# Attention's chain, a group's factor and the weight pieces moved in a one-core attention and expert kernel

## The chip, the core and the metric

One NeuronCore of a Trainium2 chip runs the whole program. Its engines are TensorE (PE, the matmuls), VectorE (DVE), ScalarE (ACT), GpSimd (POOL) and SyncE (SP, which issues nearly all DMAs here). Each engine executes its own instructions strictly in their order and waits on semaphores for the others. The metric is the device time of one execution in microseconds, the median of several runs.

## What is computed

```python
q_s = softmax(q over the 64 features of a head)
k_s = softmax(k over the 576 tokens)
x = q_s @ (k_s.T @ v)                            # 8 batches x 8 heads, 576 tokens, 64 features
xn = x / sqrt(mean(x * x) + 1e-6) * rms_g        # x as 4608 tokens x 512
y = (silu(xn @ w_gate) * (xn @ w_val)) @ w_out   # 512 -> 1536 -> 512
h = max(y @ w1, y @ w2, y @ w3)                  # 512 -> 768
out = h @ w_out2                                 # 768 -> 512
```

Everything is float32. A large product is made of three matmuls of rounded operands: the operand is split into a high part (a cast on ACT) and a low part (the difference on DVE), and high x high, low x high and high x low are added in PSUM.

## The kernel before

The 4608 tokens are nine groups of 512 (index g from 0 to 8; the last holds the tails of the 8 batches). Heads are taken in four pairs p. For each group and each of 12 feature blocks f, `iteration(g, nxt, f)` makes a gate product pg and a value product pv, 12 matmuls each (lines 598 to 600), a tanh of pg on ACT (948), the gate on DVE (949) and h on DVE (958); h goes to HBM. A group's products need its x split into xh and xl; a group's iterations therefore also do the attention of the next groups:

- the softmax of q. In groups 0 and 1 q is held by token, and `q_exp` runs eight exponentials of 128x64 on ACT with the row maximum as bias and the sum as accumulator (418). From group 2 on q is also loaded by feature (`load_by_feature`, into the tile qT): `q_exp` makes the statistics, which go through HBM (`put_stat`, `spread_stats`), `q_softmax` subtracts and multiplies on POOL with an exponential on ACT between (384 to 386), and `q_by_feature` splits the result into qh (ACT) and ql (DVE, line 100).
- `k_max`, `k_exp` (transpose pb, subtraction, exponential) and `make_kv` (pk, ten matmuls in line 453, then the scaling to kv_raw in 463 and its split).
- `make_x`: the product px of q and kv (496 to 498), scaled by the gain on ACT, squared, and the squares added on POOL (515).
- the group's factor: `token_rstd` sums the squares (548) and makes z, one over the root mean square, by three Newton steps on DVE (551 to 556). Groups 1 and 2 (`COMPACT`) spread z over the partitions with four transposes (`spread_rstd`, 571), later ones through HBM (`read_rstd`, into the tile zb of rooms_o). `normalise` multiplies x by it (580), `split_x` splits it.

Which chain step falls in which iteration is set by `turn_of(g, p)` (400), a number that counts pairs of iterations, and by the `due()` lists in `iteration`: `due(n)` holds the (g, p) whose turn is n pairs ahead. Within that a scheduler fixes the order on each engine when the program is built; the DMAs of SP stay in program order.

Beside all that, `second.advance` prepares the second layer's weights: it loads float64 words, joins them to float32 (`join`, ACT and DVE), sums them (`sums`, DVE) and writes them in quarters, called pieces below (`quarter` and `split`: a cast on ACT in line 274, a subtraction on POOL in 275, a write to w_dram by SP). It is called once per iteration from group 1 on; pieces are written in f = 0 to 9 only, except in the last group. What is left then, 13 pieces, is done by `mixture_out` (732 to 1000 us), the output stage that applies w_out by quarters with operands split in the same way (o_xh, o_xl and the like).

Of the kernel before, what the change touches and what calls it, by code (L numbers as in the profile page):

```python
# [8 lines left out]
F32 = mybir.dt.float32  # L9
# [17 lines left out]
BY_FEATURE = 2  # L27
NF1 = 12
# [26 lines left out]
def attention_moe_moe(ctx: ExitStack, tc: tile.TileContext, q, qt, k, kt, v, w1, w1_out, rms_g, w2, w2_out, out):  # L55
# [68 lines left out]
    eps = one.tile([P, LINE], F32, tag="eps", name="eps")[:, 0:1]  # L124
    nc.gpsimd.memset(eps, EPS_RMS)
# [77 lines left out]
    class Ahead:  # L203
# [5 lines left out]
        def __init__(self):  # L209
# [7 lines left out]
            self.loaded, self.st, self.now, self.apart = 0, [], 0, False  # L217
            self.issued, self.turn, self.spots = [], False, []
# [45 lines left out]
        def split(self, src, dst, name):  # L264
            if self.apart:
                self.turn = not self.turn
                t = two.tile([P, 2, N // 2], F32R, tag=("t", "qT")[self.turn], name=name, bufs=1)
            elif self.spots:
# [21 lines left out]
        def advance(self, f, last):  # L290
# [4 lines left out]
            self.apart = f is None  # L295
            room = 4 if last else 3
            while self.steps:
                step, args = self.steps[0]
                if step == self.join and self.now < self.issued[args[0]] + 2:
                    return  # L300
                writes = step == self.quarter
                cost = 0 if step == self.release else 1 if writes else 2
                if cost > room or writes and not last and f > 9:
                    return
# [94 lines left out]
    def turn_of(g, p):  # L399
        return NF1 // 2 * (g - 1) + p - (g > BY_FEATURE)  # L400

# [7 lines left out]
    def q_exp(g, p):  # L409
        qm = two.tile([P, 24], F32, tag="qm", name=f"qm_{g}_{p}")[:, 0:8]  # L410
        nc.vector.tensor_reduce(qm, q_t[g, p], axis=AX.X, op=ALU.max)
        if g < BY_FEATURE:
# [7 lines left out]
        qmax[g, p] = qm  # L420
        nc.gpsimd.tensor_sub(q_t[g, p], q_t[g, p], qm.unsqueeze(2).to_broadcast([P, 8, 64]))  # L421
        nc.scalar.activation(q_t[g, p], q_t[g, p], AF.Exp)

    def q_divide(g, p):
        qs = qsum.pop((g, p))
        nc.vector.tensor_scalar(qs, qs, EPS_SM, None, op0=ALU.add)
# [21 lines left out]
    def make_kv(g, p):  # L448
# [12 lines left out]
        for j in range(2):  # L461
            s = slice(64 * j, 64 * j + 64)
            nc.vector.tensor_scalar(raw[s, s], pk[s, s], rs[s, 0:1], None, op0=ALU.mult)
# [317 lines left out]
    def mixture_out(pr):  # L781
# [13 lines left out]
        for i, n in enumerate(OUT_ORDER1):  # L795
# [25 lines left out]
            if pr < 3 and i in (2, 4, 5, 6):  # L821
                second.advance(None, True)
# [24 lines left out]
    def iteration(g, nxt, f):  # L847
# [41 lines left out]
        if not odd:  # L889
            for t in due(-1):  # L890
                make_x(*t)
# [12 lines left out]
        else:  # L904
            for t in due(2):
                put_stat(*t, 0, qmax[t])
                load_second(*t)
# [9 lines left out]
            for t in due(0):  # L917
                q_by_feature(*t)
        if nxt is not None and nxt >= BY_FEATURE:
# [4 lines left out]
            if f == 10:  # L924
# [24 lines left out]
        nc.vector.scalar_tensor_tensor(t, t, 1.0, pg, op0=ALU.add, op1=ALU.mult)  # L949
        if ahead:  # L950
# [12 lines left out]
        if nxt in COMPACT and f == (10 if nxt < BY_FEATURE else at):  # L963
# [362 lines left out]
```

## Time and profile before

| | us |
|---|---|
| median of three runs | 1525.76 (1524.75 to 1528.61) |
| profiled execution | 1527.82, its span 1526.0 |
| TensorE busy | 1484.5 (97%) |
| DVE, ACT, POOL busy | 1060.2 (69%), 609.0 (40%), 447.6 (29%) |

A profile row names the engine, the line of the kernel, what is written from what, and in brackets how long the engine stood idle before and who released it. TensorE does its work in a fixed order, so its brackets show where the time goes that isn't matmul. The granted clock is a share of full speed; 0.5 is 1.2 GHz and 1.0 is 2.4 GHz.

### The profile page before, as it was taken

The numbers are of one execution on the slowest core, as the hardware profiler recorded it, in microseconds if no ns is written. First come the engines' busy times: TensorE is split into PE (matmuls) and PEld (weight loads), VectorE is DVE, ScalarE is ACT, GpSimd is POOL, SyncE is SP. The second block draws the span as 40 slices with busy tenths as digits, with TensorE's granted clock in tenths as the row PEclk, the third lists the DMA queues.
The fourth block names the chain that finished last, engine by engine and source line by source line (L and its number), as shares of the span: only waits on it lengthen the run. The fifth ranks groups of instructions, "written<-read, shape, count | busy, mean of one in ns | idle before, by whom it ended". The sixth has DMA issues, their size and how long they took to land. (4 is left out here: it accounts for less than half of the span.)

```text
span 1526.0 us, 19735 instructions
## 1 busy us (share of the span) xinstructions
PE 1484.5 (97%) x6692; PEld 1220.3 (80%) x6692; DVE 1060.2 (69%) x1777; ACT 609.0 (40%) x1197; POOL 447.6 (29%) x379
## 2 busy tenths in 40 slices
PE   5899999999999999999999999999999999999999
PEld 4687778887878788888867888888888888888887
DVE  6997585767576756473889989838848848847722
ACT  7754343434343433341554545413413413413311
POOL 0012443434334344441565764211111111111100
PEclk9999999999999999999999999999999999999999
DMA  8865786868686968789665154255485485485573
GB/s 273 292 196 175 224 240 197 250 213 238 201 250 210 246 195 231 238 279 348 223 235 186 60 199 174 106 199 201 165 323 199 170 321 196 167 297 202 171 264 104
DMA packets 159333, 330.30 MB, mean 216 GB/s; under 512 B 31104, under 2 KB 55680, under 8 KB 159232
## 3 DMA queue, kind: packets, MB, share of 16 engines
q1 hardware_dynamic: 155776, 322.74, 65.2%
q10 hardware_dynamic: 3456, 6.29, 1.1%
q8 instruction: 53, 0.87, 0.2%
q14 instruction: 48, 0.39, 0.1%
HBM read 246.42 MB, written 82.55 MB: 216 GB/s over the span
## 5 line engine op out<-in xcount | busy, mean ns | idle before, releaser
L1052 POOL TENSOR_TENSOR temps_wl<-temps_wl,temps_wh 128x512 f32<-128x512 f32 x36 | 48.2, 1338 | 348.8 <-ACT temps_wh L1051 282.0
L949 DVE SCALAR_TENSOR_TENSOR t<-t,pg 128x512 f32<-128x512 f32 x64 | 43.8, 684 | 62.4 <-ACT t L948 61.8
L275 POOL TENSOR_TENSOR rooms_o<-st,rooms_o 128x256 fp32r<-128x256 f32 x63 | 50.4, 807 | 113.8 <-ACT rooms_o L274 109.2
L421 POOL TENSOR_TENSOR q<-q,qm 128x512 f32<-128x512 f32 x28 | 31.1, 1112 | 175.4 <-PE pk L453 94.5
L1043 DVE TENSOR_TENSOR temps_wl<-temps_wl,p_a 128x512 f32<-128x512 f32 x72 | 49.1, 682 | 37.3 <-POOL temps_wl L1052 37.1
L1047 ACT COPY temps_wh<-p_G 128x512 f32<-128x512 f32 x36 | 21.1, 586 | 105.8 <-PE p_G L606 105.5
L604 PE MATMUL p_a<-x_wh,chunk 128*128 128x512 f32 x160 | 62.3, 389 | 0.0
L605 PE MATMUL p_a<-x_wl,chunk 128*128 128x512 f32 x160 | 62.3, 389 | 0.0
L606 PE MATMUL p_a<-x_wh,chunk 128*128 128x512 f32 x160 | 62.3, 389 | 0.0
L605 PE MATMUL p_a<-x_wh,chunk 128*128 128x512 f32 x160 | 62.2, 389 | 0.0
L604 PE MATMUL p_a<-x_wl,chunk 128*128 128x512 f32 x160 | 62.2, 389 | 0.0
L606 PE MATMUL p_a<-x_wl,chunk 128*128 128x512 f32 x160 | 62.2, 389 | 0.0
L958 DVE SCALAR_TENSOR_TENSOR h<-t,pv 128x512 f32<-128x512 f32 x66 | 45.0, 682 | 24.7 <-PE pv L600 22.3
L1049 DVE TENSOR_TENSOR temps_wl<-temps_wh,p_V 128x512 f32<-128x512 f32 x36 | 24.6, 683 | 43.9 <-PE p_V L606 43.9
L948 ACT ACTIVATE t<-pg 128x512 f32<-128x512 f32 x64 | 37.8, 590 | 39.4 <-PE pg L600 38.8
L755 POOL TENSOR_TENSOR h_X<-h_Y,h_X 128x512 f32<-128x512 f32 x24 | 41.7, 1747 | 28.4 <-DVE o_ql L100 12.4
L949 DVE SCALAR_TENSOR_TENSOR rooms_o<-rooms_o,pg 128x512 f32<-128x512 f32 x42 | 28.5, 678 | 28.8 <-ACT rooms_o L948 28.8
L757 POOL TENSOR_TENSOR h_Y<-h_W,h_Y 128x512 f32<-128x512 f32 x24 | 39.0, 1639 | 25.3 <-DMA h_W<-h_dram 24.9
L453 PEld LDWEIGHTS pk<-v,k 128*128 128x128 f32 x300 | 39.7, 200 | 7.5 <-issue 2.4
L453 PE MATMUL pk<-v,k 128*128 128x129 f32 x300 | 41.2, 285 | 4.4 <-DMA v<-in_v 2.2
L759 POOL TENSOR_TENSOR h_Z<-h_Z,h_X 128x512 f32<-128x512 f32 x24 | 40.0, 1685 | 11.0 <-DVE h_X L752 8.4
L948 ACT ACTIVATE rooms_o<-pg 128x512 f32<-128x512 f32 x42 | 24.8, 590 | 42.5 <-PE pg L600 42.4
(1227 smaller groups left out, 5001.7 us busy)
## 6 DMA issues: line engine op xcount, KB each, us to landing
chunk<-w_dram SPq DMA_DIRECT2D x112, 768.0 KB, 4.3
h_dram<-h SPq DMA_DIRECT2D x108, 256.0 KB, 3.6
w_dram<-rooms_o SPq DMA_DIRECT2D x95, 256.0 KB, 3.0
stat<-stats SPq DMA_DIRECT2D x112, 128.0 KB, 5.1
words<-in_w SPq DMA_DIRECT2D x24, 512.0 KB, 6.6
chunk<-w_dram SPq DMA_DIRECT2D x48, 256.0 KB, 3.7
k<-in_k SPq DMA_DIRECT2D x30, 320.0 KB, 4.5
v<-in_v SPq DMA_DIRECT2D x30, 320.0 KB, 5.9
```

What stands on the lines that cost most here:

```text
L275: nc.gpsimd.tensor_sub(t[:, 1, :], src, t[:, 0, :].bitcast(F32))
L453: nc.tensor.matmul(pk[:, 0 : P + 1], k_t[g, p][:, c, :], v_t[g, p][:, c, :], start=(c == 0), stop=(c == 4))
L604: nc.tensor.matmul(pt, ah, bh, start=first, stop=False, skip_group_check=onto)
L605: nc.tensor.matmul(pt, ah, bl, start=False, stop=False, skip_group_check=onto)
L606: nc.tensor.matmul(pt, al, bh, start=False, stop=last, skip_group_check=onto)
L755: nc.gpsimd.tensor_sub(x, y, x)
L759: nc.gpsimd.tensor_sub(z, z, x)
L948: nc.scalar.activation(t, pg, AF.Tanh, scale=0.5)
L949: nc.vector.scalar_tensor_tensor(t, t, 1.0, pg, op0=ALU.add, op1=ALU.mult)
L958: lows.append(nc.vector.scalar_tensor_tensor(h, t, 0.5, pv, op0=ALU.mult, op1=ALU.mult))
L1043: nc.vector.tensor_add(y, x, pt)
L1052: nc.gpsimd.tensor_add(w, u2, s5)
```

## The change

Four things are done. At the start, pairs 1 and 3 of group 0 (`AT_ONCE`) get their exponential in one instruction behind a subtraction on POOL, with the sum taken by a reduction on DVE; group 0's scaling to kv_raw goes from DVE to ACT; and a small exponential at the very start replaces a constant. From group 3 on `turn_of` is one smaller, and the lists are changed so that `make_x` stays where it was while `q_by_feature` comes half a pair earlier. Group 2's factor is spread and applied between pg and pv of f = 10 instead of at the end of f = 9. And pieces are written in every f, with none left to the output stage.

```diff
+AT_ONCE = ((0, 1), (0, 3))
...
-    eps = one.tile([P, LINE], F32, tag="eps", name="eps")[:, 0:1]
-    nc.gpsimd.memset(eps, EPS_RMS)
+    warm = one.tile([P, LINE], F32, tag="warm", name="warm")[:, 0:1]
+    nc.scalar.activation(warm, ones_f[:, 0:1], AF.Exp)
...
-        def advance(self, f, last):
+        def advance(self, last):
...
-                if step == self.join and self.now < self.issued[args[0]] + 2:
+                if step == self.join and (args[0] >= self.loaded or self.now < self.issued[args[0]] + 2):
                     return
-                writes = step == self.quarter
-                cost = 0 if step == self.release else 1 if writes else 2
-                if cost > room or writes and not last and f > 9:
+                cost = 0 if step == self.release else 1 if step == self.quarter else 2
+                if cost > room:
                     return
...
     def turn_of(g, p):
-        return NF1 // 2 * (g - 1) + p - (g > BY_FEATURE)
+        return NF1 // 2 * (g - 1) + p - 2 * (g > BY_FEATURE)
...
     def q_exp(g, p):
...
-        if g < BY_FEATURE:
+        if g < BY_FEATURE and (g, p) not in AT_ONCE:
...
+        if g < BY_FEATURE:
+            qsum[g, p] = two.tile([P, 8], F32, tag="qs", name=f"qs_{g}_{p}")
         nc.gpsimd.tensor_sub(q_t[g, p], q_t[g, p], qm.unsqueeze(2).to_broadcast([P, 8, 64]))
         nc.scalar.activation(q_t[g, p], q_t[g, p], AF.Exp)
 
     def q_divide(g, p):
         qs = qsum.pop((g, p))
+        if (g, p) in AT_ONCE:
+            nc.vector.tensor_reduce(qs, q_t[g, p], axis=AX.X, op=ALU.add)
...
-            nc.vector.tensor_scalar(raw[s, s], pk[s, s], rs[s, 0:1], None, op0=ALU.mult)
+            if g == 0:
+                nc.scalar.activation(raw[s, s], pk[s, s], AF.Copy, scale=rs[s, 0:1])
+            else:
+                nc.vector.tensor_scalar(raw[s, s], pk[s, s], rs[s, 0:1], None, op0=ALU.mult)
...
-            if pr < 3 and i in (2, 4, 5, 6):
-                second.advance(None, True)
...
         if not odd:
+            for t in due(-2):
+                if t[0] > BY_FEATURE:
+                    make_x(*t)
             for t in due(-1):
-                make_x(*t)
+                if t[0] > BY_FEATURE:
+                    q_by_feature(*t)
+                else:
+                    make_x(*t)
...
             for t in due(2):
                 put_stat(*t, 0, qmax[t])
-                load_second(*t)
+                if t[0] < NB:
+                    load_second(*t)
...
             for t in due(0):
-                q_by_feature(*t)
+                if t[0] == BY_FEATURE:
+                    q_by_feature(*t)
+                if t[0] == NB:
+                    load_second(*t)
...
-            if f == 10:
+            if f == 10 and nxt > BY_FEATURE:
                 for p in range(4):
                     normalise(nxt, p)
...
         nc.vector.scalar_tensor_tensor(t, t, 1.0, pg, op0=ALU.add, op1=ALU.mult)
+        if nxt == BY_FEATURE and f == 10:
+            spread_rstd(nxt)
+            for p in range(4):
+                normalise(nxt, p)
...
-        if nxt in COMPACT and f == (10 if nxt < BY_FEATURE else at):
+        if nxt == 1 and f == 10:
             spread_rstd(nxt)
...
-            second.advance(f, nxt is None)
+            second.advance(nxt is None)
```

What this does to the orders is shown at three places.

ACT at the start of the program; q_0 to wh_0_3 are the q of group 0's four pairs, k and wl hold k, pk and px are banks. Before:

```order
L418 ACTIVATE q_0_219,qs_0_269<-q_0_219,qm_0_267 128x64 x8
L418 ACTIVATE q_1_229,qs_1_287<-q_1_229,qm_1_285 128x64 x2
L444 ACTIVATE k_0_221<-k_0_221 128x640
L418 ACTIVATE q_1_229,qs_1_287<-q_1_229,qm_1_285 128x64 x6
L444 ACTIVATE k_1_231<-k_1_231 128x640
L418 ACTIVATE wh_0_2_239,qs_2_305<-wh_0_2_239,qm_2_303 128x64 x8
L444 ACTIVATE wl_0_2_241<-wl_0_2_241 128x640
L418 ACTIVATE wh_0_3_249,qs_3_327<-wh_0_3_249,qm_3_325 128x64 x8
L444 ACTIVATE wh_0_3_251<-wh_0_3_251 128x640
```

and after:

```order
L126 ACT_TABLE_LOAD
L126 ACTIVATE warm<-ones_f 128x1
L414 ACTIVATE q_0_219,qs_0_269<-q_0_219,qm_0_267 128x64 x8
L420 ACTIVATE q_1_229<-q_1_229 128x512
L444 ACTIVATE k_0_221<-k_0_221 128x640
L488 COPY qh_0_369<-pt_0_364 128x512
L444 ACTIVATE k_1_231<-k_1_231 128x640
L414 ACTIVATE wh_0_2_239,qs_2_298<-wh_0_2_239,qm_2_296 128x64 x8
L444 ACTIVATE wl_0_2_241<-wl_0_2_241 128x640
L464 ACTIVATE kv_raw_213<-pk_0_328,kr_0_336 64x64 x2
L488 COPY qrts<-pt_1_398 128x512
L420 ACTIVATE wh_0_3_249<-wh_0_3_249 128x512
```

Two pairs' eight exponentials became one instruction each, and group 0's kv_raw scalings (L464) stand on ACT among them.

PE around the factor of group 2 (z_2, the four transposes named rstd), in the iterations f = 9 and 10 of group 1. Before:

```order
L599 MATMUL pv_9_2060<-x_2_1398,wh_(1, 9)_1196 128x512
L600 MATMUL pv_9_2060<-x_2_1398,wl_(1, 9)_1215 128x512
L571 MATMUL rstd_2075<-ident,z_2_2033 128x128 x4
L453 MATMUL pk_0_2094<-v_0_223,k_0_1899 128x129 x5
L598 MATMUL pg_10_2124<-x_0_1390,wh_(1, 10)_1260 128x512
L599 MATMUL pg_10_2124<-x_0_1390,wh_(1, 10)_1260 128x512
```

and after, from the last matmuls of pg of f = 10:

```order
L601 MATMUL pg_10_2157<-x_2_1386,wh_(1, 10)_1248 128x512
L602 MATMUL pg_10_2157<-x_2_1386,wh_(1, 10)_1248 128x512
L603 MATMUL pg_10_2157<-x_2_1386,wl_(1, 10)_1267 128x512
L574 MATMUL rstd_2173<-ident,z_2_2071 128x128 x4
L601 MATMUL pv_10_2183<-x_0_1378,wh_(1, 10)_1248 128x512
L602 MATMUL pv_10_2183<-x_0_1378,wh_(1, 10)_1248 128x512
```

The transposes moved from ahead of pk and pg of f = 10 to behind that pg.

DVE at the end of the third group (g = 2): xraw is normalised (L580, after the change L583) with the factor in a tile of rooms_o, then split into the tiles x. Before:

```order
L949 SCALAR_TENSOR_TENSOR t_10_2877<-t_10_2877,pg_10_2864 128x512
L580 TENSOR_TENSOR xraw_0_2233<-xraw_0_2233,rooms_o_1432 128x512
L580 TENSOR_TENSOR xraw_1_2373<-xraw_1_2373,rooms_o_1432 128x512
L580 TENSOR_TENSOR xraw_2_2490<-xraw_2_2490,rooms_o_1432 128x512
L580 TENSOR_TENSOR xraw_3_2606<-xraw_3_2606,rooms_o_1432 128x512
L958 SCALAR_TENSOR_TENSOR h_10_2893<-t_10_2877,pv_10_2880 128x512
L376 TENSOR_REDUCE qs_2_2910<-q_2_2725 128x8
L443 TENSOR_TENSOR k_1_2771<-k_1_2771,pb_1_2915 128x640
L377 TENSOR_SCALAR qs_2_2910<-qs_2_2910 128x8
L100 TENSOR_TENSOR ql_0_2920<-qT_0_2721,qh_0_2919 128x512
L379 RECIPROCAL qr_2_2913<-qs_2_2910 128x8
L100 TENSOR_TENSOR x_0_2923<-xraw_0_2233,x_0_2923 128x512
```

and after:

```order
L960 SCALAR_TENSOR_TENSOR rooms_o_1421<-rooms_o_1421,pg_11_2990 128x512
L583 TENSOR_TENSOR xraw_0_2286<-xraw_0_2286,rooms_o_1420 128x512
L583 TENSOR_TENSOR xraw_1_2402<-xraw_1_2402,rooms_o_1420 128x512
L583 TENSOR_TENSOR xraw_2_2518<-xraw_2_2518,rooms_o_1420 128x512
L583 TENSOR_TENSOR xraw_3_2620<-xraw_3_2620,rooms_o_1420 128x512
L101 TENSOR_TENSOR x_0_2979<-xraw_0_2286,x_0_2979 128x512
L101 TENSOR_TENSOR x_1_2982<-xraw_1_2402,x_0_2979 128x512
L101 TENSOR_TENSOR x_1_2982<-xraw_2_2518,x_1_2982 128x512
L435 TENSOR_REDUCE km_3_2968<-kT_3_2911 128x1
L101 TENSOR_TENSOR x_2_2987<-xraw_3_2620,x_2_2987 128x512
L973 SCALAR_TENSOR_TENSOR h_11_3018<-rooms_o_1421,pv_11_3005 128x512
L101 TENSOR_TENSOR ql_1_3037<-rooms_o_1422,qh_1_3036 128x512
```

Normalise stood behind the gate of pg_10 and stands behind that of pg_11 now; ql of the next group's pair 1, which before came in f = 1 directly ahead of its product, follows h_11. At the end of the sixth group the order changes in the same way; at those of the fourth and fifth normalise stands one or two operations later than before, ahead of the gate of pg_11.

## Rows read from the trace of the kernel before

**Rows 1.** the page's busy time of each engine, its share of the span, and instructions
```profile
PE 1484.5 (97%) x6692; PEld 1220.3 (80%) x6692; DVE 1060.2 (69%) x1777; ACT 609.0 (40%) x1197; POOL 447.6 (29%) x379
```

**Rows 2.** what PE waited for: us in total, times, longest
```profile
PE rstd L571 <- DVE z L556: 5.2, 2, 2.7
...
PE px L497 <- DVE ql L100: 4.0, 7, 0.9
...
PE pv L548 <- POOL sacc L515: 1.0, 1, 1.0
```

**Rows 3.** stretches: PE, PEld, DVE, ACT, POOL busy; PEclk, DMA share, GB/s
```profile
0.00:60.00 60.00, 40.94 (x195) 31.17 (x196) 46.46 (x117) 45.25 (x147) 1.59 (x18) 0.94 0.82 279
60.00:115.00 55.00, 53.32 (x250) 41.68 (x248) 53.08 (x109) 35.06 (x86) 5.05 (x4) 1.00 0.71 224
118.00:121.00 3.00, 3.00 (x9) 2.30 (x8) 2.84 (x5) 2.24 (x4) 0.00 (x0) 0.51 0.23 87
193.00:196.00 3.00, 3.00 (x16) 2.91 (x14) 2.54 (x5) 1.67 (x3) 2.16 (x2) 0.52 0.83 300
```

**Rows 4.** timeline of ACT, POOL, DVE; start, duration, then the instruction; POOL's row is a summary
```profile
17.82 0.35 ACT L418 ACTIVATE wh<-wh,qm 128x64 f32<-128x64 f32 x1 [1.92 <-DVE qm L415]
...
20.49 0.72 ACT L444 ACTIVATE wh<-wh 128x640 f32<-128x640 f32 x1
...
L421 POOL TENSOR_TENSOR q<-q,qm x28: 1042/1045/1561, 96.7 to 594.1; 128x512 f32<-128x512 f32 x28
...
19.68 0.58 DVE L463 TENSOR_SCALAR kv_raw<-pk,kr 64x64 f32<-64x64 f32 x2
```

**Rows 5.** timeline of PE and DVE, 22 to 60 us
```profile
22.80 1.91 PE L494 MATMUL px<-qh,kv_raw 128*128 128x512 f32 x2
...
58.21 0.67 DVE L194 TENSOR_TENSOR wl_(1, 3)_772<-y,wh_(1, 3)_753 128x512 fp32r<-128x512 f32 x1
...
59.42 0.40 PE L600 MATMUL pg<-xh,wl_(1, 3)_772 128*128 128x512 f32 x1
```

**Rows 6.** timeline of DVE, POOL and PE, 114 to 118 us
```profile
114.32 1.20 DVE L556 SCALAR_TENSOR_TENSOR z<-a,z 128x4 f32<-128x4 f32 x1
...
116.43 0.15 DVE L556 SCALAR_TENSOR_TENSOR z<-a,z 128x4 f32<-128x4 f32 x1
...
114.23 1.27 POOL L386 TENSOR_TENSOR qT<-qT,stat 128x512 f32<-128x512 f32 x1
...
117.32 0.62 PE L571 MATMUL rstd<-ident,z 128*128 128x128 f32 x4 [2.49 <-DVE z L556]
```

**Rows 7.** timeline of DVE and PE, 187 to 197 us
```profile
187.38 0.75 DVE L435 TENSOR_REDUCE km<-kT 128x1 f32<-128x576 f32 x1 [2.68 <-DMA kT<-in_kt]
...
189.58 0.39 PE L600 MATMUL pv<-x,wl_(1, 9)_1215 128*128 128x512 f32 x1
192.71 0.69 PE L571 MATMUL rstd<-ident,z 128*128 128x128 f32 x4 [2.75 <-DVE z L556]
...
196.60 0.40 PE L598 MATMUL pg<-x,wh_(1, 10)_1260 128*128 128x512 f32 x1
```

**Rows 8.** timeline of PE, the last of seven waits of one kind
```profile
527.63 0.50 PE L497 MATMUL px<-ql,kvh 128*128 128x512 f32 x1 [0.94 <-DVE ql L100]
```

**Rows 9.** timeline of DVE and PE at the ends of two groups
```profile
283.42 1.88 DVE L100 TENSOR_TENSOR x<-xraw,x 128x512 fp32r<-128x512 f32 x3
...
285.93 0.39 PE L598 MATMUL pg<-x,wh_(1, 0)_518 128*128 128x512 f32 x1
...
651.78 0.69 DVE L580 TENSOR_TENSOR xraw<-xraw,rooms_o 128x512 f32<-128x512 f32 x1 [1.23 <-DMA rooms_o<-rstd]
```

**Rows 10.** timeline of PE and ACT in the output stage, first and last of seven waits
```profile
764.78 0.50 PE L605 MATMUL o_acc<-o_spare,w1q_wl 128*128 128x512 f32 x1 [0.23 <-DVE o_spare L100]
...
782.70 0.47 PE L604 MATMUL o_acc<-o_qh,w1q_wl 128*128 128x512 f32 x1 [0.61 <-ACT o_xraw L99]
...
769.07 0.42 ACT L274 CAST wq<-st 128x256 fp32r<-128x256 f32 x1 [4.75 <-DMA w_dram<-wq]
```

More of the change, by code (lines that the diff above doesn't have):

```diff
@@ L216, in __init__ @@
                 self.sources += [w2_out[fp, i] for i in range(2)]
-            self.loaded, self.st, self.now, self.apart = 0, [], 0, False
-            self.issued, self.turn, self.spots = [], False, []
+            self.loaded, self.st, self.now = 0, [], 0
+            self.issued, self.spots = [], []
             self.free, self.held, self.last = [(None, 0), (None, 0)], [], False
@@ L264, in split @@
         def split(self, src, dst, name):
[L265 to L268, printed above, removed]
+            if self.spots:
                 t = self.spots.pop(0)
@@ L294, in advance @@
             self.load()
-            self.apart = f is None
             room = 4 if last else 3
@@ L997, in attention_moe_moe @@
         sp(dst, src)
+    assert not second.steps, len(second.steps)
     prepare(0, 1)
@@ L1001, in attention_moe_moe @@
         if pr == NPAIR - 1:
-            assert not second.steps, len(second.steps)
             load_raw(0)
```

## The prediction

> **What bounds the kernel now.** I read the page's busy line first: TensorE is busy for 97% of the span [rows 1], so a change counts only where TensorE waits, or where it runs at its lower clock. The list of what TensorE waited for comes next [rows 2]: two long waits for a group's factor (rstd), seven waits for the low half of the softmaxed q (px for ql), and one for a sum of squares on POOL. Then the stretches by clock [rows 3]: in the 3 us around and after the two rstd waits the granted clock is 0.51 and 0.52, the 1.2 GHz level, so each of those waits is paid a second time. The rest is the start, where TensorE is busy for 40.9 of the first 60 us [rows 3], and the beginning of the output stage [rows 10]. Durations are of the profiled execution, 1527.82 us, which is 2.06 above the median 1525.76; the sum is taken from 1527.82 and the same 2.06 is taken off at the end.
>
> **Half of group 0's q at once.** For pairs 1 and 3 the eight exponentials of 128x64 with their accumulator reads go. A pair's eight run from 17.82 to 20.49 on ACT, 2.67 us [rows 4]. In their place stand a POOL subtraction of 1.05 us [rows 4], one exponential of 128x512 (no such row at the start; between 0.35, a 128x64 one, and 0.72, a 128x640 one [rows 4]; I take 0.6, nearer the size) and a DVE reduction of as many elements, about 0.6. The kv_raw scalings of four pairs, 0.58 us a pair on DVE [rows 4], become eight 64x64 scalings on ACT, at most 0.35 each by the 128x64 row; I take 0.3. ACT: 2 x (2.67 - 0.6) - 8 x 0.3 = 1.7 us less. DVE: 4 x 0.58 - 2 x 0.6 = 1.1 us less. At first the gain is larger than these, since kv_raw no longer queues behind DVE's other work and the next bank comes free with it. Following the new orders by hand with the durations of the rows, the first px starts near 18.3 instead of 22.80 [rows 5], 4.5 us sooner. That isn't kept: the order puts the low half of feature 3's weights on DVE behind some 4.6 us of word joins. It was done at 58.21 + 0.67 = 58.88 with TensorE using it at 59.42 [rows 5]; by hand it is now done near 59.5 while TensorE arrives near 57.3, a new wait of about 2 us. I get 2.8 us at the start of feature 4, and take 2.3 for a lower clock that such a wait may bring. Bounds: 0, if DVE's work sets the end of this stretch, and 4.0.
>
> **The factor of the group after it.** TensorE waited 2.49 us at 117.32 for z on DVE [rows 6]. The new order has one DVE operation of 0.6 us fewer between the variance and the last z. I take 0.6; bounds 0 and 4.2, which is the whole wait and the half-clock loss behind it (1.7, next part).
>
> What sets that wait in the trace is POOL: three POOL operations run there, and a z step on 128x4 takes 1.20 us beside the last of them and 0.15 two microseconds later [rows 6]. The Trainium skill (SBUF — State Buffer, Who interferes with whom) says that a VectorE instruction with two SBUF inputs contends with a GpSimd instruction that reads SBUF, and that whoever issues first holds the shared pair; the trace agrees, with its 1.20 against 0.15. By that rule each of the change's two new POOL subtractions could hold up a DVE operation by as much as it runs itself, and the sum would be some 2.1 us smaller. The rival "nothing from the start" carries that chance.
>
> **The third group's factor later.** Its four rstd matmuls stood at the head of feature 10; now they stand between that feature's pg and pv. z was late because DVE had stood 2.68 us for a kT load [rows 7]. TensorE waited 2.75 from the end of the ninth pv, whose last matmul starts at 189.58, to 192.71 [rows 7]; the clock then stays at 0.52 for 193 to 196 [rows 3] and is full again at 196.60 [rows 7]: 3 x 0.48 + 0.6 x 0.5 = 1.7 us lost. Together 4.5. In the new order TensorE comes to rstd after pk and twelve more matmuls, some 3.8 us of work at full clock (estimated at 0.23 a matmul), so near 193.6, a microsecond behind the time at which z let rstd start. What is late next is normalise and the split of xl on DVE, which start 1 to 2 us later and by hand still end 1.5 us ahead of their first use. Bounds: 2.75 (the clock falls elsewhere instead) and 5.0.
>
> **The chain a step sooner.** From the fourth group on, loads, statistics, k's exponential, pk and kv come one pair of features sooner, q_by_feature half a pair sooner, and make_x stays. The last and largest of the seven waits, 0.94 [rows 8], is far smaller than half a pair (24 matmuls, about 5.5 us), so all seven go: 4.0 [rows 2]. POOL's sum of squares no longer stands behind a subtraction of q: 1.0 [rows 2], taken as 0.9 since another operation may follow it. Together 4.9; bounds 3.0 (ql of some pairs lands behind other DVE work) and 5.9 (a wait of pk for k's exponential goes too). The chain's DMAs move along: the feature-major q of the pair after next now waits on SP until ql has been read, since it fills the same tile; what stands behind it on SP are piece writes and the next loads, all due a pair later.
>
> Against it stands what the order does at the ends of the third and the sixth group: normalise and xl come behind pg_11's gate on DVE, no longer ahead of the tenth product's h. Before, the last xl ended at 283.42 + 1.88 = 285.30, and TensorE's fourth slice began at 285.93, its low part one matmul later [rows 9]: a cover of 0.9 us. By hand the last xl now ends 7.1 us after pg_11 and TensorE comes to it 7.2 after: about even. I take 0.35 of wait at each, -0.7; bounds 0 and -7, for which see the last rival.
>
> **Pieces done by the output stage.** 13 weight pieces (an ACT cast, a POOL subtraction and an SP write each) leave the output stage; features 10 and 11 of groups 1 to 7 get up to three each. In the output stage ACT waited 4.75 us before the cast of a piece, for the write of an older one, with four o_xh casts behind it [rows 10]. Seven TensorE waits, from the 0.23 at 764.78 to the 0.61 at 782.70 [rows 10], come to 3.31. The last of them follows a wait of ACT for TensorE itself and stays. I take 2.7; bounds 1.0 and 3.3. In the groups the pieces lie beside matmuls, on engines with gaps; I take 0, bound -2.
>
> **Sum.** 2.3 + 0.6 + 4.5 + 4.9 - 0.7 + 2.7 = 14.3 us. 1527.8 - 14.3 = 1513.5, and with the 2.06 off, **1511.5 us** as the median. Within 0.3%, 4.6 us, is about what a measurement of this kernel can't tell from no change.
>
> **Rivals.**
> *Nothing from the start.* DVE is busy for 53.1 of the 55 us from 60 to 115 [rows 3] and the change frees only 1.1 us of it; if that sets the start of feature 8 the 2.3 are gone, and so they are if POOL's subtractions stretch DVE's work: 1513.8. For it: the 0.5 us of cover at 58.88 [rows 5]. Against: DVE idles for 13.5 of the first 60 us [rows 3].
> *The next factor is freed too.* If POOL's three operations no longer meet the z steps, the whole 2.49 and its half clock go: 3.6 more, 1507.9. For it: one stretched step alone costs 1.05 [rows 6]. Against: that chain is not moved by the change.
> *A part does nothing.* The output stage's waits may come from DVE's splits, which get no faster, or ql may still be late: 2.7 to 4 less, 1514.2 to 1515.5. For it: the first of the seven names DVE, not ACT [rows 10].
> *The factor lands late at the ends of groups: slower.* Six times the next group's factor is read through SP, behind the piece writes of feature 9, of which there are now more. DVE already waited 1.23 for that read at 651.78 [rows 9], where nothing hung on it. If it lands d later than DVE wants it, TensorE waits d at the two ends that have no cover and about d - 2 at the four others, each with about 1.7 of half clock as at [rows 7]. Against the 15.0 gained elsewhere that is even at d = 2.1; at d = 4 it is 2 x 5.7 + 4 x 3.7 = 26.2 and the time 1525.8 + 11.2 = 1537.0. Against: in four of the six DVE didn't wait for the read at all.
>
> **How the numbers follow.** Forecast 0.50, nothing from the start 0.14, the next factor 0.08, a part does nothing 0.10; late factors 0.18, of which 0.11 with small d at some ends (1521 to 1530) and 0.07 beyond. Faster by over 0.3% 0.82, within 0.3% 0.11, slower 0.07. The range leaves out the late factors alone. Its low end is the next factor with the start's upper bound (1.7) and the chain's and the output stage's (1.0 + 0.6): 1507.9 - 3.3 = 1504.6. Its high end is nothing from the start, a part that does nothing and 2 us of price for the pieces: 1513.8 + 2.7 + 2.0 = 1518.5, say 1519.
>
> **What would show it.** In the changed kernel's trace: no px wait for ql after 290 us; no rstd wait, and a granted clock of 1.0, between 190 and 200 us; the first px near 18.3 and a wait of about 2 us at feature 3; no ACT cast of a piece after 735 us, and TensorE's waits from 764 to 783 us under 0.8 in all; near 285 and 520 us waits for xl under 0.5. I am wrong if such waits come back under another name (normalise, xl, xh), or if the granted clock falls where it did not before.

## The result and the profile after

The changed kernel took 1512.50 us as the median of six runs (1509.65 to 1517.33), against 1526.02 of before on the same chip: ratio 0.9913, 95% interval 0.9892 to 0.9934, 13.5 us less. On a second chip it was 0.9902 (0.9880 to 0.9923). The prediction, 1511.5, was met within 1.0 us, and its range held; several of its terms were not met, and they cancelled.

The profiled execution took 1514.36 us, span 1512.2 (before: 1527.82 and 1526.0). Line numbers moved with the change: 571 is 574 now, 453 stays, 598 to 600 are 601 to 603, 580 is 583, 418 and 422 are 414 and 420, and 274 is 272. First the page's busy line, which answers to [rows 1]:

```profile
PE 1479.8 (98%) x6692; PEld 1220.0 (81%) x6692; DVE 1059.5 (70%) x1769; ACT 611.0 (40%) x1176; POOL 446.6 (30%) x380
```

TensorE is busy for 4.7 us less and the span is 13.8 shorter, so 9.1 us are waits. What it waited for (us, times, longest), which answers to [rows 2]:

```profile
PE pk L453 <- ACT k L444: 2.3, 2, 1.8
PE rstd L574 <- DVE z L559: 2.2, 1, 2.2
PE pg L602 <- DVE xl L101: 1.5, 2, 1.0
...
PE pg L602 <- DVE x L101: 1.3, 1, 1.3
```

The px waits for ql and the second rstd wait are gone. The waits for the low half of x grew, and so did those of pk for k's exponential, which before are in its list as

```profile
PE pk L453 <- ACT k L444: 1.3, 2, 0.9
```

Where the lead came from, by the starts of the same matmuls in the two timelines (us; the lead, in brackets, is by how much the changed kernel is sooner):

```
start of                    before     after
feature 8, group 0           96.39     95.70   (0.69)
feature 0, group 1          124.96    122.41   (2.55)
feature 10, group 1         195.20    189.20   (6.00)
feature 0, group 2          208.71    203.63   (5.08)
feature 0, group 7          589.92    583.50   (6.42)
output stage, first o_acc   727.91    721.48   (6.43)
end of the span            1526.0    1512.2   (13.8)
```

Between groups 1 and 7 these marks also hold work that the sooner chain does ahead (a pk more or less before a mark is 1 us); at group 7, where the chain has ended, they don't. Over half of the lead comes in the output stage, and from group 2 to group 7, where the chain was to bring nearly 5 us, it grows by 1.3. These are marks of one execution: in a second profile of the changed kernel (below) the lead is 2.26 at feature 8, 9.84 at group 7 and 17.2 at the end, so a mark carries a scatter of some 3 us.

Why, the rows at the end of the fifth group show (timeline of SP, DVE and PE, then a stretch with the granted clock behind the fifth busy time):

```profile
414.40 1.38 SPq L143 DMA_DIRECT2D w_dram<-rooms_o  x3
...
417.81 3.91 SPq L143 DMA_DIRECT2D stat<-stats  x4
421.77 0.58 SPq L143 DMA_DIRECT2D rooms_o<-rstd  x1
...
427.59 2.50 DVE L583 TENSOR_TENSOR xraw<-xraw,rooms_o 128x512 f32<-128x512 f32 x4 [2.35 <-DMA rooms_o<-rstd]
...
432.58 2.36 PE L453 MATMUL pk<-v,k 128*128 128x129 f32 x10 [1.79 <-ACT k L444]
...
433.00:436.00 3.00, 3.00 (x13) 2.73 (x12) 3.00 (x5) 1.09 (x3) 0.36 (x1) 0.50 0.99 321
```

The read of the next group's factor stands on SP behind three writes of pieces, 1.38 us, and four loads of statistics, which hold the queue for 3.91 us. It is issued at 421.77, and DVE stands 2.35 us until 427.59 for it, with k's subtraction behind. So k's exponential is late, pk waits 1.79, and the next 3 us run at a granted clock of 0.50. [rows 9] had DVE waiting for the same read, with nothing behind it.

At the end of the third group, which answers to the other rows of [rows 9] (DVE, then PE):

```profile
277.88 0.69 DVE L960 SCALAR_TENSOR_TENSOR rooms_o<-rooms_o,pg 128x512 f32<-128x512 f32 x1 [1.55 <-ACT rooms_o L959]
278.48 2.49 DVE L583 TENSOR_TENSOR xraw<-xraw,rooms_o 128x512 f32<-128x512 f32 x4
280.89 1.89 DVE L101 TENSOR_TENSOR x<-xraw,x 128x512 fp32r<-128x512 f32 x3
...
279.87 0.50 PE L601 MATMUL pg<-x,wh_(1, 0)_506 128*128 128x512 f32 x1 [0.18 <-ACT x L100]
281.63 0.50 PE L602 MATMUL pg<-x,wh_(1, 0)_506 128*128 128x512 f32 x1 [1.25 <-DVE x L101]
```

Normalise follows the gate of pg_11 at once, and TensorE waits 0.18 and 1.25 for the split. At the start the answer to [rows 5] is this (PE, then ACT):

```profile
10.54 1.09 PE L479 MATMUL pt<-ident,q 128*128 128x128 f32 x4 [5.53 <-ACT q L420]
...
19.74 1.04 PE L497 MATMUL px<-qh,kv_raw 128*128 128x512 f32 x2
...
59.46 0.50 PE L601 MATMUL pg<-xh,wh_(1, 3)_741 128*128 128x512 f32 x1 [1.08 <-ACT wh_(1, 3)_741 L190]
...
60.88 0.50 PE L603 MATMUL pg<-xh,wl_(1, 3)_760 128*128 128x512 f32 x1 [0.18 <-DVE wl_(1, 3)_760 L195]
...
16.65 0.62 ACT L464 ACTIVATE kv_raw<-pk,kr 64x64 f32<-64x64 f32 x2
```

The first px starts at 19.74, 3.1 us sooner, although TensorE had stood 5.53 us for the first q that it transposes. The scalings on ACT take 0.62 a pair. Feature 3 comes with new waits: 1.08 for the high half of its weights, cast on ACT, and 0.18 for the low half on DVE. Just before, at 54.92, TensorE waits 1.02 for xl, where the kernel before waits 0.42.

### The profile page after: what moved, and what is told of

The parts are those of the page before. It is cut to its first block, busy times and chain, and to the rows that moved or that the text cites. A ratio compares the mean times of both kernels' runs of the same rounds, so it can differ in the third digit from the quotient of the medians.

```text
span 1512.2 us, 19762 instructions
## 1 busy us (share of the span) xinstructions
PE 1479.8 (98%) x6692; PEld 1220.0 (81%) x6692; DVE 1059.5 (70%) x1769; ACT 611.0 (40%) x1176; POOL 446.6 (30%) x380
## 4 chain that ended last, share of the span: by engine, by line
PE 70%; DVE 6%; DMA 3%; issue 2%; ACT 1%; SPq 1%; POOL 1%; DVEq 0%; POOLq 0%
PE p_a L608 4%; PE p_a L607 4%; PE p_a L609 4%; PE pg L602 4%; PE pg L601 4%; PE pg L603 4%; PE pv L603 4%; PE pv L602 4%; PE pv L601 4%; PE o_acc L608 3%; PE o_acc L609 3%; PE o_acc L607 3%; PE p_G L607 2%; PE p_G L608 2%; PE p_G L609 2%; PE o_a L607 2%
## 5 line engine op out<-in xcount | busy, mean ns | idle before, releaser
L273 POOL TENSOR_TENSOR rooms_o<-st,rooms_o 128x256 fp32r<-128x256 f32 x77 | 65.0, 852 | 126.3 <-ACT rooms_o L272 119.7
L272 ACT CAST rooms_o<-st 128x256 fp32r<-128x256 f32 x77 | 31.8, 423 | 39.8 <-DMA w_dram<-rooms_o 16.1
```

Of the source, the lines that this page charges most:

```text
L273: nc.gpsimd.tensor_sub(t[:, 1, :], src, t[:, 0, :].bitcast(F32))
```

## The experiments

Parts 1 to 4 are the start, the chain, the third group's factor and the pieces. Ratios are to the kernel before on the same chip, with 95% intervals; 0.001 is 1.5 us. The kernel without three POOL operations ran once and stands below.

```
                                     ratio    interval
all four                            0.9913   0.9892 to 0.9934
all four, second chip               0.9902   0.9880 to 0.9923
without the start                   0.9905   0.9889 to 0.9920
without the chain                   0.9998   0.9984 to 1.0011
without the third group's factor    0.9926   0.9910 to 0.9941
without the pieces                  0.9925   0.9909 to 0.9942
the chain alone                     0.9945   0.9931 to 0.9959
the third group's factor alone      1.0001   0.9987 to 1.0014
the pieces alone                    1.0002   0.9985 to 1.0018
all four, early read                0.9884   0.9867 to 0.9900
without the start, early read       0.9890   0.9875 to 0.9906
all four, early read, PSUM steps    0.9864   0.9843 to 0.9886
```

### Each part undone

**The start undone.**

```diff
-AT_ONCE = ((0, 1), (0, 3))
...
-            if g == 0:
-                nc.scalar.activation(raw[s, s], pk[s, s], AF.Copy, scale=rs[s, 0:1])
-            else:
-                nc.vector.tensor_scalar(raw[s, s], pk[s, s], rs[s, 0:1], None, op0=ALU.mult)
+            nc.vector.tensor_scalar(raw[s, s], pk[s, s], rs[s, 0:1], None, op0=ALU.mult)
```

> The changed kernel with its first part undone: group 0's q again by eight exponentials per pair, kv_raw scaled on DVE, the old constant instead of the early exponential. Theory A (from the marks in the two traces, where feature 8 of group 0 starts 0.7 us sooner after the change): the start is bound by DVE's work between 40 and 100 us, and undoing costs 0.7 us, about 1513. Theory B (the prediction's term): undoing costs 2.3 us, about 1515, with feature 4 starting near 68.6 and feature 8 near 96.4 instead of 95.7. In both the half clock from 18 to 26 us comes back; under A it costs nothing at feature 8.

Measured: 1512.47, ratio 0.9905, no slower than with the part. The half clock from 18 to 26 us is back, and feature 8 starts at 96.27, 0.57 later than in the first profile of the changed kernel. That is nearer theory A, but the times don't tell the two theories apart: their 0.7 and 2.3 us differ by 0.001, and each interval reaches at least 0.0015 to either side. Two of the waits at the ends of groups, near 281 and 511 us, are not there in this kernel, although the factor is read as late as in the changed one; pk still waits 1.71 at 431.82. What takes the two away is open.

**The chain undone.**

```diff
-        return NF1 // 2 * (g - 1) + p - 2 * (g > BY_FEATURE)
+        return NF1 // 2 * (g - 1) + p - (g > BY_FEATURE)
```

(with the lists of `iteration` as before).

> The changed kernel with its second part undone: the attention chain one step later again from the fourth group on. Theory A (marks: between group 2 and group 7 the change's lead grew by 0.6 us only, and the wait for POOL's sum of squares near 183 us was worth 1.1): new waits for k's exponential and for xl at the ends of groups took back what the seven px waits gave; undoing costs 1 to 2 us, 1513.5 to 1514.5, the px waits for ql come back with about 4 us in all and the waits near 281, 432 and 511 us go. Theory B (the prediction): undoing costs 4.2 us, about 1516.7, since the waits at the ends of groups come from the pieces and stay.

Measured: 1528.25 against 1527.80, ratio 0.9998. Both theories fall: not 1 to 4 us but the whole gain is lost. What TensorE waited for:

```profile
PE px L500 <- DVE ql L101: 7.1, 9, 1.9
...
PE px L499 <- ACT qh L100: 2.9, 3, 1.5
PE px L495 <- ACT qh L387: 2.7, 1, 2.7
```

With the pieces in features 10 and 11 and the chain where it was, px waits 12.7 us for q, against 4.0 in [rows 2] and, with the chain and the pieces both changed, 0.4 for qh and none for the split to ql.

**The third group's factor undone.**

```diff
-            if f == 10 and nxt > BY_FEATURE:
+            if f == 10:
...
-        if nxt == BY_FEATURE and f == 10:
-            spread_rstd(nxt)
-            for p in range(4):
-                normalise(nxt, p)
...
-        if nxt == 1 and f == 10:
+        if nxt in COMPACT and f == (10 if nxt < BY_FEATURE else at):
             spread_rstd(nxt)
```

> The changed kernel with its third part undone: the third group's factor is spread at the head of feature 10 again. Theory A (the prediction): the wait and the half clock behind it come back, 4.5 us, about 1517. Theory B: the other parts have by themselves brought z sooner (its last step ends at 189.8 us in the changed kernel, with the ninth value product over at 188.2), so the wait comes back with 1.6 us only, 1514 with the clock kept and 1515.7 with it lost.

Measured: 1514.97, ratio 0.9926, 2 us more than with the part by the ratios, within their intervals. The rstd wait came back with 0.36 us, less than even theory B said (PE, DVE, POOL):

```profile
192.87 0.62 PE L574 MATMUL rstd<-ident,z 128*128 128x128 f32 x4 [0.36 <-DVE z L559]
...
191.07 1.26 DVE L557 SCALAR_TENSOR_TENSOR a<-z 128x4 f32<-128x4 f32 x1
...
191.03 1.28 POOL L382 TENSOR_TENSOR qT<-qT,stat 128x512 f32<-128x512 f32 x1 [2.11 <-ACT qT L381]
```

DVE stands for no load here, and one z step is stretched, to 1.26, beside a POOL operation.

**The pieces undone.** The limit to f up to 9 and the calls in `mixture_out` are back.

```diff
-                if cost > room:
+                if cost > room or writes and not last and f > 9:
                     return
...
+            if pr < 3 and i in (2, 4, 5, 6):
+                second.advance(None, True)
```

> The changed kernel with its fourth part undone: no pieces in features 10 and 11, and 13 pieces in the output stage again. Theory A (marks: from the first o_acc to the end the lead grew from 6.4 to 13.8 us): undoing costs 7.3 us, about 1519.8, with TensorE's listed waits between 750 and 820 us back at about 4.8 us and the rest in gaps too short to be listed. Theory B (the prediction's term): 2.7 us, about 1515.2, the waits near 804 us being DVE's own work. Under both, if the pieces of features 10 and 11 are what makes the waits at the ends of groups, those waits are gone here and the cost is smaller by up to 3 us.

Measured: 1515.73, ratio 0.9925: 1.8 us more than with the part by the ratios, between the theories. Two large amounts stand behind it. From the start of group 1, before which no piece is done, to the first o_acc this kernel's lead over before grows by 11.6 us (from -0.33 to 11.27), the changed kernel's by 3.9 (from 2.55 to 6.43) in its first profile and by 7.3 in its second. Without the pieces of features 10 and 11 the waits at the ends of groups are gone but for one of 0.28 at 430. Then the output stage has its waits again, as in [rows 10], and the lead grows there by 0.9 only, against 7.4 in the changed kernel. So 6.4 are gained there by the part, for 7.7 or 4.3 paid in the groups, by the profile; the 1.8 of the times lies between. At the end of the fifth group the factor is read sooner (SP):

```profile
412.62 0.37 SPq L143 DMA_DIRECT2D w_dram<-rooms_o  x1
...
414.70 2.55 SPq L143 DMA_DIRECT2D stat<-stats  x4
```

One piece write stands ahead of it and not three, and the loads of statistics take 2.55 us and not 3.91. It is issued at 417.30, and DVE doesn't wait for it.

### Parts alone

**The chain alone** (the kernel before with the edits of `turn_of` and of the lists).

```diff
-        return NF1 // 2 * (g - 1) + p - (g > BY_FEATURE)
+        return NF1 // 2 * (g - 1) + p - 2 * (g > BY_FEATURE)
```

> The kernel before with the second part alone: the attention chain one step sooner from the fourth group on, all else as before. Theory A (from the run with the third part undone, where the wait for the third group's factor was only 0.36 us without that part): the sooner chain brings the kT loads sooner, so DVE no longer stands 2.7 us at 187 us and the factor's wait goes by itself, 4 us, beside the seven px waits, 4.0, and POOL's sum, 1.0; with 1 us of new waits at the ends of groups that is 8 us less than before. Theory B (the prediction's terms): the factor's wait of 2.75 with its half clock stays, and the gain is 4.2 us. The piece waits of the output stage stay under both.

Measured: 1518.04 against 1526.86, ratio 0.9945, 8.4 us less, the size of theory A without its mechanism. The factor's wait stayed (PE, then DVE and a stretch of the clock):

```profile
191.39 0.67 PE L571 MATMUL rstd<-ident,z 128*128 128x128 f32 x4 [2.49 <-DVE z L556]
...
187.83 1.21 DVE L555 TENSOR_TENSOR a<-a,var 128x4 f32<-128x4 f32 x1
...
189.94 1.11 DVE L555 TENSOR_TENSOR a<-a,var 128x4 f32<-128x4 f32 x1
...
192.00:194.00 2.00, 2.00 (x12) 2.00 (x10) 2.00 (x4) 0.95 (x2) 0.00 (x0) 0.50 1.15 370
```

DVE no longer stands for the kT load [rows 7], but two z steps take 1.21 and 1.11: the wait has another cause and nearly the same size. From group 2 to group 7 the chain alone gains 6.6 us (374.6 against 381.2), of which about 1 is work that it did before the first of these marks: from group 1 to group 2 its lead falls by 0.2, although POOL's wait of 1.0 is gone. The listed px waits there were 4.0, and one pk wait of 0.42 is new. The rest is not in the list: a matmul behind a wait is followed by the next after 0.34 us, not 0.23, and there are gaps too short to be listed. The mean time from one px matmul to the next, listed waits left out, falls from 0.268 to 0.232 over 57 of them, 2.1 us.

**The third group's factor alone**, the edits shown above in the other direction, on the kernel before.

```diff
+        if nxt == BY_FEATURE and f == 10:
+            spread_rstd(nxt)
```

> The kernel before with the third part alone: the third group's factor between the gate and value products of feature 10. Theory A (the prediction): 4.5 us less than before, no rstd wait and no half clock between 190 and 200 us. Theory B (as in the run with this part undone, where the wait was 0.36 us): the part alone is worth under 1.5 us, since a later stage takes the time back.

Measured: 1528.90 over 12 runs against 1528.62, ratio 1.0001: nothing. In the profile the wait and its half clock are gone from where they were, and a half clock stands a little earlier, behind the wait of 0.95 for POOL's sum (PE; stretches):

```profile
183.04 1.05 PE L548 MATMUL pv<-ones_f,sacc 128*128 128x1 f32 x8 [0.95 <-POOL sacc L515]
...
186.00:188.00 2.00, 2.00 (x6) 1.60 (x5) 1.71 (x3) 0.00 (x0) 0.00 (x0) 0.50 1.05 293
190.00:200.00 10.00, 10.00 (x53) 8.37 (x52) 7.65 (x16) 5.01 (x11) 5.63 (x5) 1.00 0.96 255
```

This profile is of the shortest of the 12 executions, 1522.78. What takes the gain back in the others can't be seen in it, and stays open.

**The pieces alone.**

```diff
-                if cost > room or writes and not last and f > 9:
+                if cost > room:
                     return
...
-            if pr < 3 and i in (2, 4, 5, 6):
-                second.advance(None, True)
```

> The kernel before with the fourth part alone: pieces in every feature, none left to the output stage. Theory A (from the run with the chain undone, whose px waits for qh and ql came to 12.7 us): the pieces of features 10 and 11 hold up qh and ql on ACT and DVE, the groups take 8 to 12 us more, the output stage 7.4 less, together 1 to 5 us slower than before. Theory B (the prediction's terms): the groups take nothing more, 2.7 to 7.4 us faster.

Measured: 1529.42 against 1528.62, ratio 1.0002: no difference that these runs can tell, which leaves room for the lower end of theory A's loss and none for theory B. px waits 8.5 us for q in all, more than before's 4.0, and in the output stage the lead over before grows by 7.3. One of its waits, followed back (PE, ACT, POOL, SP):

```profile
394.11 0.49 PE L491 MATMUL px<-qh,kvh 128*128 128x512 f32 x1 [1.06 <-ACT qh L99]
...
393.44 0.62 ACT L99 CAST qh<-qT 128x512 fp32r<-128x512 f32 x1 [0.92 <-POOL qT L381]
...
390.08 1.29 POOL L379 TENSOR_TENSOR qT<-qT,stat 128x512 f32<-128x512 f32 x1 [3.91 <-DMA stat<-stats]
392.12 1.29 POOL L381 TENSOR_TENSOR qT<-qT,stat 128x512 f32<-128x512 f32 x1 [0.74 <-ACT qT L380]
...
383.73 3.40 SPq L142 DMA_DIRECT2D stat<-stats  x4
```

px waits for qh, ACT for the multiplication on POOL, and POOL for the statistics that SP loads. In this chain nothing has room from the load of the statistics to px; what the pieces do to this load is not shown.

### Versions that test the new waits

**The factor read first.** The changed kernel with one move:

```diff
+        if nxt is not None and nxt > BY_FEATURE and f == at + 2:
+            read_rstd(nxt)
         for dst, src in later:
             sp(dst, src)
...
-            if f == at + 2 and nxt not in COMPACT:
-                read_rstd(nxt)
```

> The changed kernel with one edit: the read of the next group's factor through SP is issued first in feature 9, ahead of the stores, the piece writes and the four statistic loads, not last. Theory A (the read lands late: DVE waited 2.35 us for it at 427.59, with k's subtraction, k's exponential on ACT and pk queued behind): normalise moves back ahead of pg_11's gate, the waits near 281, 432 and 511 us (1.4, 1.8 and 0.5) go and so does the half clock at 433 to 437: 5 us less than the changed kernel. Theory B: only the wait at 432 hangs on the read, since at the end of the third group it had landed before the gate; 2 to 3.5 us less, the waits near 281 and 511 stay.

Measured: 1508.51, ratio 0.9884, less than the changed kernel by 4.4 us from its first ratio (0.9913) and by 2.8 from its second (0.9902); the intervals overlap. All three waits are gone, as theory A said; the size doesn't decide between the theories. The wait of pk is the one that shows what the read does: it stands in both profiles of the changed kernel (1.79, 1.56) and in the one without the start (1.71), and it is gone here and in the next run. At the end of the fifth group (SP, then DVE):

```profile
409.69 0.33 SPq L143 DMA_DIRECT2D rooms_o<-rstd  x1
...
415.00 0.64 DVE L583 TENSOR_TENSOR xraw<-xraw,rooms_o 128x512 f32<-128x512 f32 x1
...
416.16 2.44 DVE L583 TENSOR_TENSOR xraw<-xraw,rooms_o 128x512 f32<-128x512 f32 x3
```

The read is issued 12 us sooner, normalise runs in feature 10, and from group 2 to group 7 this kernel takes 373.9 us (changed 379.9 and 377.5 in its two profiles, before 381.2).

**The same without the start** (`AT_ONCE` and the scaling on ACT undone, as above).

> The early read of the run before, and the first part undone (group 0's q by eight exponentials per pair, kv_raw scaled on DVE). If the start is worth 0.7 us, 0.7 more than with the early read alone; if the start's part costs something later, as the run with that part undone hinted (its lead at group 6 was 9.5 us against 6.4), 1 to 3 us less.

Measured: 1509.85, ratio 0.9890, against 0.9884 with the start. With and without the early read, the part at the start makes no difference that these runs can tell.

**Without three POOL operations.** The changed kernel, which leaves out three operations on q and so doesn't compute the softmax of two pairs in full.

```diff
-        nc.gpsimd.tensor_sub(qT[g, p], qT[g, p], m)
+        if (g, p) != (2, 0):
+            nc.gpsimd.tensor_sub(qT[g, p], qT[g, p], m)
```

(and likewise the multiplication, and the subtraction of `q_exp` for (2, 1)).

> The changed kernel, leaving out three POOL operations: the subtraction and the multiplication of q by feature for group 2's pair 0, and the subtraction in the exponential of its pair 1. They are the three that run beside the Newton steps of group 1's factor near 111 to 115 us. Theory A (the engines hold each other up): the steps of 0.97 to 1.25 us shrink to 0.15 to 0.2, z ends some 3 us sooner and the rstd wait of 2.2 us at 116 goes. Theory B: the steps are late for DVE's other work; they stay long or the wait stays over 1.5.

Measured in one execution: 1509.78. The steps take 0.16 and the wait is gone, as theory A said. The changed kernel (DVE, POOL, PE, and the stretch after it):

```profile
113.33 1.21 DVE L559 SCALAR_TENSOR_TENSOR z<-a,z 128x4 f32<-128x4 f32 x1
...
113.24 1.28 POOL L382 TENSOR_TENSOR qT<-qT,stat 128x512 f32<-128x512 f32 x1
...
116.35 0.62 PE L574 MATMUL rstd<-ident,z 128*128 128x128 f32 x4 [2.21 <-DVE z L559]
...
116.00:119.00 3.00, 2.65 (x14) 2.21 (x15) 2.81 (x7) 1.24 (x3) 0.00 (x0) 1.00 0.23 87
```

and without the three (DVE, PE):

```profile
111.03 0.16 DVE L562 SCALAR_TENSOR_TENSOR z<-a,z 128x4 f32<-128x4 f32 x1
...
113.58 0.60 PE L577 MATMUL rstd<-ident,z 128*128 128x128 f32 x4
```

**The steps with one input in PSUM**, on top of the early read:

```diff
+            if g == 1:
+                var = pv[:, 4:8]
...
+            if g == 1:
+                nc.vector.scalar_tensor_tensor(a, z, 0.25**i, var, op0=ALU.mult, op1=ALU.mult)
+                nc.vector.tensor_mul(a, z, a)
```

(The intermediate a lies in the bank of pv, too. The other groups keep their steps.)

> The changed kernel with the early read, and the Newton steps of group 1's factor rewritten so that each has one input in PSUM and one in SBUF (the variance and the intermediate stand in PSUM; as many operations). Theory A (two SBUF inputs collide with POOL's reads): no step is stretched beyond 0.3 us beside POOL's operations, the rstd wait near 116 falls from 2.2 to under 0.5, and the half clock after it goes: 2 to 4 us less than the early read alone, near 1505.5. Theory B (POOL holds DVE up whatever the operands, or the steps wait for each other longer in PSUM): steps of about 1 us remain and the wait stays over 1.5; the same time as the early read alone.

Measured: 1507.18, ratio 0.9864, the lowest of all; beside it on the same chip the changed kernel took 1513.35 (0.9902). Its first half is as theory A said (DVE, POOL, PE):

```profile
114.72 0.16 DVE L562 SCALAR_TENSOR_TENSOR pv<-z,pv 128x4 f32<-128x4 f32 x1
114.91 0.17 DVE L563 TENSOR_TENSOR pv<-z,pv 128x4 f32<-128x4 f32 x1
...
118.13 0.69 DVE L968 SCALAR_TENSOR_TENSOR t<-t,pg 128x512 f32<-128x512 f32 x1 [2.46 <-ACT t L967]
...
119.33 0.16 DVE L567 SCALAR_TENSOR_TENSOR z<-pv,z 128x4 f32<-128x4 f32 x1
...
114.09 1.85 POOL L380 TENSOR_TENSOR qT<-qT,stat 128x512 f32<-128x512 f32 x1 [12.76 <-DMA stat<-stats]
...
119.64 0.62 PE L582 MATMUL rstd<-ident,z 128*128 128x128 f32 x4 [1.81 <-DVE z L567]
```

Beside a POOL subtraction that runs from 114.09 to 115.94 the steps take 0.16 and 0.17. The second half of theory A did not come true: a gate stands between the steps in DVE's order, DVE waits 2.46 us for that gate's tanh, and TensorE still waits 1.81. The two profiles bear out what the Trainium skill (SBUF — State Buffer, Who interferes with whom) states: a VectorE instruction with two SBUF inputs contends with a GpSimd instruction that reads SBUF, and one with at most one SBUF input doesn't, outside VectorE's 2-port modes. A gain over the early read alone (0.9884) is not shown, since the intervals overlap.

**The changed kernel again.**

> The changed kernel once more, beside the others on one chip. Two of its six earlier runs took 1514 to 1517 us with a mean clock of 0.997 and three 1510 with 1.0. Theory A: its time differs by whether the clock falls at the two waits of about 2 us (rstd near 116, pk near 432), worth some 1.7 us each; the profile shows as many half-clock stretches as its mean clock says. Theory B: the difference lies in DMA times, with equal clocks.

Measured: 1513.35 (1510.99 to 1518.99). In its first six runs the three of 1509.65 to 1510.64 have a mean clock of 1.0 and the two of 1515.90 and 1517.33 one of 0.997; in the second six the longest, 1518.99, has 0.995. A stretch at half clock that costs 1.7 us lowers the mean by 0.0011, so 0.003 of clock would be 4.5 of the 6.3 us between the two sets of the first six: theory A holds there in part. It doesn't hold in the second six, whose shortest run, 1510.99, has a clock of 0.998 and the four behind it 0.998 to 0.999. Nor does it explain the two profiles, which have one such stretch each after the start and differ by 3.4 us. In this profile the wait for group 1's factor is followed by one, in the first it was not (PE, stretch):

```profile
114.76 1.09 PE L574 MATMUL rstd<-ident,z 128*128 128x128 f32 x4 [2.17 <-DVE z L559]
...
116.00:118.00 2.00, 2.00 (x7) 1.44 (x6) 1.50 (x3) 1.24 (x3) 0.00 (x0) 0.50 0.35 131
```

The kernel before hardly follows its mean clock in the 23 runs beside this one (1524.1 to 1534.7), so the clock isn't all that differs between executions. What else does is open.

## Why the prediction was right, and where it was wrong

The total was right: 14.3 us forecast, 13.5 measured. By its steps:

- **The start, 2.3: not settled.** The first px came at 19.74, not 18.3. The wait of 2 us that was to come at feature 3, for the low half of its weights on DVE, is 0.18; in its place TensorE waits 1.08 for the high half on ACT and 1.02 for xl. The lead is 1.4 at feature 4 and 0.69 at feature 8 in the first profile, 2.1 and 2.3 in the second. Over the eight profiles that hold the part feature 8 starts between 94.13 and 99.37, over the six that don't between 96.27 and 102.69, and three of the eight fall to the half clock near 30 us. Undone, it changes nothing that these runs can tell. So the rival "nothing from the start" is neither shown nor excluded.
- **The next factor, 0.6: mis-sized.** The wait fell by 0.28. The marks give 1.9 in the first profile, since no half clock followed there; in the second profile one did. The rival's mechanism is shown: without POOL's three operations the wait goes.
- **The third group's factor, 4.5: right in the profile, wrong as a price.** There is no wait and a clock of 1.0, and from feature 9 of group 1 to feature 0 of group 2 the lead grew by 3.5. But alone the part measures nothing, and undone it costs about 2, within the intervals, with a wait of 0.36 left. The step that failed took the wait as fixed: it was a load in [rows 7], two stretched steps with the chain alone, and one in the whole.
- **The chain, 4.9 less 0.7: wrong twice.** The seven px waits went, and alone the chain gives 8.4. In the first profile of the changed kernel the ends of groups took back not 0.7 but waits of 1.25, 0.18, 1.79 and 0.51 with a half clock of 1.7, together 5.4; a wait of 0.94 of pk that before has at 423.62 went, as the upper bound had it. The last rival had the mechanism, the factor read behind other DMAs, with the piece writes ahead of it. What stood ahead were the piece writes, 1.38 us, and the loads of statistics, 3.91, which the rival did not name; with the pieces undone the two take 0.37 and 2.55 and DVE doesn't wait. It came at one end in full, and the early read removes it.
- **The pieces, 2.7 and a price of 0: mis-sized on both sides.** In the output stage the changed kernel gains 7.4, of which 0.9 comes without the part: the two waits of 0.7 that before has after 816 us went too, and so did that of 0.61 at 782.70, which was to stay, and gaps too short to be listed. In the groups the price was 7.7 by the first profile and 4.3 by the second, with the chain sooner; with the chain where it was, the pieces cost as much as they gave.
- **The sum: terms that don't add.** The chain alone is worth 8.4, the factor and the pieces alone nothing, and without the chain the other three together nothing. The chain gives the pieces their room. That the total agreed is chance. By the marks of the first profile, 2.9 was forecast up to group 1 and 2.6 came; 8.7 was forecast from there to the output stage and 3.9 came; 2.7 was forecast in the output stage and 7.4 came. So 4.8 too much stood against 4.7 too little.

Of the signs named ahead, those on px's waits for ql, on rstd between 190 and 200 us, on ACT's casts and on the waits from 764 to 783 us came; the bound of 0.5 at the ends of groups did not hold (1.25 and 0.51), and the granted clock fell at one place where it had not before, 433 us.

## What to carry to other kernels

Price parts that share a chain together: a move that gives slack is worth more than the waits that it removes, since it decides what another move costs. When a chain is moved, look at what stands in the DMA queue ahead of the one small read that the next stage needs; that read at the head of its iteration gave about 3 to 4 us here, at the limit of what these runs can tell. One profile can't price a part worth 2 us: the marks of two executions of the same kernel differ by more. Before designing around a wait for a short serial computation, see whether another engine stretches its steps.

## What the runs showed of the hardware

- A DVE operation on 128x4 takes 0.15 to 0.17 us alone and 0.97 to 1.26 beside a POOL operation, if its inputs lie in SBUF; with one input in PSUM two such steps beside a POOL operation took 0.16 and 0.17.
- The clock fell to half behind a wait of 1.79 in one execution and not behind one of 2.21 in the same; in another execution it fell behind 2.17 at the second place and not behind 1.56 at the first.
- The changed kernel differs by up to 8 us between executions on one chip (1510.99 to 1518.99); by the mean clocks, half-clock stretches can be a part of that; the rest stays open.
- Listed waits understate what they cost: the output stage gained 7.4 where 4.8 were listed, and against the kernel with the pieces undone 6.4 where 4.1 were.
